# Output projection of a gated MLP: seven half-size block products per pair of token tiles, replaced by plain products

## The chip, the cores and the metric

The kernel runs on one core of a Trainium2 chip. Its time is the device time of one execution in microseconds (us); before the change it is 233.87 us, the median of three runs (233.48 to 234.02). A core has a matrix engine (TensorE, PE in the profile), three engines for elementwise work (VectorE is DVE, ScalarE is ACT, GpSimd is POOL), and SyncE (SP), which here only issues DMA transfers. The engines run side by side and wait for one another through semaphores. TensorE multiplies a 128x128 stationary block by a moving block of up to 512 columns and adds the result up in PSUM, which has eight banks of 128 x 512 fp32.

## The reference, cut to what matters

S = 2048 tokens, D = 512, gate width Fh = 896. The first half is a linear attention block, the second a gated MLP with a spatial mixing matrix:

```python
x = A_x
h = x + A_ref(layernorm(x), A_wqkv, A_wo)           # linear attention, 32 heads of 16
# B_ref(layernorm(h), ...):
z  = gelu(einsum('bsd,df->bsf', x, w_in))           # [S, 2*Fh]
z1 = z[..., :Fh]
z2 = layernorm(z[..., Fh:])
g  = einsum('ts,bsf->btf', w_sp, z2) + b_sp[None, :, None]
return einsum('bsf,fd->bsd', z1 * g, w_out)         # the output projection
# result: h + B_ref(layernorm(h), ...)
```

The change concerns the last line alone: [2048, 896] times [896, 512], added to h.

## The kernel before

The kernel is a list of operations for the five engines, each with what it reads and writes. Dependencies and semaphores are worked out from these. The order on each engine comes from a packed string, `ORDER`, which lists all operations in one fixed sequence that was found for this version of the kernel.

The output is made in 16 token tiles of 128 rows. Fh = 896 is KF = 7 contraction chunks of 128, so a plain tile takes seven products with a 512-column moving operand. The kernel before does only two of the 16 tiles plainly (`mo`). The other 14 are done two at a time (`mo_pair`). A pair, two halves of D and two groups of contraction chunks make a 2x2 by 2x2 block product; it is computed with seven block products in place of eight, by the Winograd form of Strassen's scheme. Each block product has 256 columns. HF = 3 chunks (or 2, parameter `nk`) are in each block; the rest of the seven chunks is done plainly.

The scheme needs sums and differences of blocks of the weights (`wout_sums`) and of the gated activations (`z1_sums`), made on VectorE. Partial products that go into two outputs are carried from one half of a bank to another by a ScalarE copy:

```python
def z1_sums(j, tg, nk, n):
    ...
    combine(us[0], x21, x22, ALU.add)
    combine(us[1], us[0], x11, ALU.subtract)
    combine(us[2], x11, x21, ALU.subtract)
    combine(us[3], x12, us[1], ALU.subtract)
    return us

def mo(n, banks):                                     # one tile, plain
    w = D // len(banks)
    for j, b in enumerate(banks):
        ...
        parts = ((0, 3, 6, 1, 4), (2,), (5,))
        for i, fcs in enumerate(parts):
            matmuls(bank(b, w), [(z1T[:, fc, n * P:(n + 1) * P], wout[:, fc, cs]) for fc in fcs], ...)
        dve(lambda v, o=o, b=b: v.tensor_tensor(o, bank(b, w), o, ALU.add), ...)
        store(n, cs, o, "SP" if j == 0 else "ACT")

def mo_pair(tg, i, us, nk, X, Y, tm):                 # two tiles, banks X and Y
    ...
    matmuls(X0, [(z1T[:, c, ta], wout[:, c, d0]) for c in ks])
    matmuls(X1, [(u1[:, c, ti], v1[:, c, :]) for c in ks], **onto)
    act(Y1, X0, ACT.Copy, DH2)
    for t, n in zip(tm, (a, b)):
        dve(lambda v, t=t, n=n: v.tensor_tensor(t, X1, h[:, n, d1], ALU.add), ...)
    matmuls(X0, [(z1T[:, HF + c, ta], wout[:, HF + c, d0]) for c in ks], **onto)
    matmuls(Y1, [(u2[:, c, ti], v2[:, c, :]) for c in ks], **onto)
    act(X1, Y1, ACT.Copy, DH2)
    matmuls(Y1, [(u3[:, c, ti], v3[:, c, :]) for c in ks], **onto)
    act(Y0, Y1, ACT.Copy, DH2)
    matmuls(X1, [(u4[:, c, ti], wout[:, HF + c, d1]) for c in ks], **onto)
    matmuls(Y0, [(z1T[:, HF + c, tb], v4[:, c, :]) for c in ks], **onto)
    rest = [(2 * HF,)] if nk == HF else [(2 * HF,), (HF - 1,), (KF - 2,)]
    for fcs in rest:
        for q, t in ((X, ta), (Y, tb)):
            matmuls(bank(q), [(z1T[:, fc, t], wout[:, fc, :]) for fc in fcs], **onto)
    # then four VectorE additions of 256 columns into h, and two stores
```

The projection follows the spatial mixing, which runs in two passes `p`. Each pass makes the gated activations of two groups of four tiles (`tg = p` and `p + 2`), itself with seven block products in place of eight (`cell`, 512 columns each), on PSUM banks 0 to 5:

```python
for p in range(NG // 2):
    ... # last chunk (banks 4 and 5), sums t1, t2, t4 on VectorE, three cells
    if p == 0:
        wout_sums()
        for j, tg in enumerate((0, 2)):
            us = z1_sums(j, tg, HF, 2)
            for i in (0, 1):
                mo_pair(tg, i, us, HF, 6, 7, tmp[0])
us = z1_sums(3, 3, HF - 1, 2)
mo_pair(3, 0, us, HF - 1, 6, 7, tmp[0])
mo_pair(3, 1, us, HF - 1, 0, 1, tmp[1])
us = z1_sums(2, 1, HF - 1, 1)
mo_pair(1, 0, us, HF - 1, 2, 3, tmp[2])
mo(5, (4,))
mo(7, (5, 6))
```

At its start the kernel keeps TensorE busy with products of a zero block, whose results are not used: 34 at once, and 16 more behind the statistics of the first x tile. The program with the change has these too, in the same form.

Of the kernel before, what the change touches and what calls it, by code (L numbers as in the profile page):

```python
# [6 lines left out]
FP32 = mybir.dt.float32  # L7
# [4 lines left out]
P = 128  # L12
GRAN = 16
EARLY = 1
SEM_NS = 45.0
ORDER = "c-jrogMttU00qE@tj)G<d$VoZwz=81ZQHhO+jiZ}FH8U;Aqt`)I$|IuVj(u-pq}C*0RSQ#Lc$1!;0TQ{2mv8HA|f)PA}*335t1S?k|8-#ASH4k4{{?fQXwDmqYx^h0Mep7Dxm@zp$Xz4AyT6-(x3=3pdiwr7&0L}0+A6#kr|EA6qQj0&Cnbz(E?SG1zC{|HIN;}(G}fM0zJ?TB~cAIP#rZ<8*NYvtxyVeP#0rR8f7pJV=*4}P#;UM6wA;SIZ+nn&>pSP4n5Heeb5`B5CLH^0TVF^lhGdo&=>tM1s%`;4KWA<F%5&!5zEmD2XP385riQ)f)!YaRalLqIEE8Aj^P-Abr^{?IE_&ljj5Q9&gg=fn1T6NfLS<+g;<ZZIE6EKhUa*R7kG-<n1i7hh7H(=MOchY*n#cXj4hapdDw%!*oj@(jdM7Qeb|o!*otkqiYqve3%H0&xQWZShFiFf8+eUZc!RgNjeEF{JGhGn2+oHH!H|r=06s!QzQcPw#uNO+Cw#yUe8gvb!7qHpH^ks~{6S3q`@g)t8Ym1yF)Twf79%qfqcAGtF*f5e4#P7Xe<Ky6F*P$Y53?{j^D;jRFb&f(9n&)dGcps+tRxFEA4{<`|3b{h?99QO3}hh|W)T);E(T*w)?ryDU^&KTLM~wo7Gnw4Wi2LR875|VR$xU|VoTOzZB}L#)@K7YWFt1_V&>)=u4QZXVs}<$b+%z|E@fM`ViPuF4>nYBmSl1!WfCT13Z`Uo?co-tP*3h<A1>n*4rOY!V|#YsKCa__PGw3pWi{4db2d^MrP6vH;4pS%CoX4Su3$fQ<py?Uf3D;J4&)#PF}*S<tuiZ}wlbrpa|APKII}3LvTGZ&DW`HMmvSqwy0EcEas~&p8;7uonyQ(atA$#smGUT`@~fZ<sE`6xSfe<NGg(B%bcRJ$Ld8`|C3TjiRYpg6ly`WAcX^C&SWZ{@gxC0%<yBTs`G<e`j9>Vb-?*KlxskKDgF88!b2yjtxQSypmg6{{tGJ5?xsVe$pVxVuhj@dNc#rRRj^}xwhk28?c$=Gff+zW&7x;nCd5RzTf-m`r-}#UK_v!(E@F5p*0Vi`JE2)CQtD+*PvRW&d+NiDCsl7U=qdKXxx~PhRD}(~{nX9>*5%rT7`HQdkn~x|x=4n<_JXKXl#a9j0RCOiLYhGd~MN&dtW;8`tBE^suT45Ack(F3U6h*-lQ?Zm(;S^P|6-RN^Uv*SVGqg&*)kgy~NK-UeGgVhXnysPgs^RLU?pmu68mQG8qG1}Pahk4?nyT^Yrw!_%zUrxITBie=pt+i*(dwmn8l(AIpoJQ%Ihv?RO5({{qNQ4-Wm>O|+N{OeqHU_J<=U<_+N7;op_SU9ojRx#-m4SZrG473BRZ<%I;oUCrFcH9LprV9+M_f2pks>fq&}y!I<H*5pi8=<)K1{*x~6o#sLQ&etGcUOx~Y50?Sy`ykNT|p`lMt|<VSj_w0^8-dZHIf<yU&G41TKTdZ{n^s&{&;^!}#r`k};5<1EhVU;3$x{;hxdBl@rMI=O>6o9#@7<<Jh}0uJdA4(rSg=kU(&07r0kM|2biI+`Onvhz5HV>qYtIjW;OjtjZ43%aO_IHpUun2Wov>$#yDxuj#ev75N5OS`#yx|f@|tjoBCd%M2-x`F$+rCYhb`?<B-xUC0xpa*%d%ejJsJk&$n&J|tB<z3lTT-~KS!BsuclU>7;T+_8&&9&X$9o*5w-N~KZ#ob-UQ#{qvJj@%t$(udWBRtD9Jl&(c#oav0<2=?gy~eXW$Md|_>pa&ByvR$u-t)cCi@ns#z09k;(%Zb<JG|336w1N<UT+lFU42_y9m``p-aWj*E4<pf{2yF?$Zh"


class _Op:
# [233 lines left out]
def bass_sequential_preLN__linear_attn_block__mixer_gmlp__prompt_kernel(  # L253
# [14 lines left out]
    H = 32  # L268
# [115 lines left out]
    def bank(b, n=512, lo=0):  # L384
        return psum[:, b, lo:lo + n]
# [8 lines left out]
    def matmuls(out_ap, pairs, start=True, stop=True, onto=False, **k):  # L394
        n = out_ap.free_size() if callable(getattr(out_ap, "free_size", None)) else out_ap.shape[-1]

        kw = {"skip_group_check": True} if onto else {}

        def fn(pe):
            inst = None  # L400
            for i, (a, b) in enumerate(pairs):
                inst = pe.matmul(out_ap, lhsT=a, rhs=b, start=start and i == 0, stop=stop and i == len(pairs) - 1, **kw)  # L402
            return inst
        return PE(fn, [a for p in pairs for a in p], [out_ap], len(pairs) * max(65.0, n / 2.4 + 2.5), **k)
# [26 lines left out]
    def dma(eng, out_ap, in_ap, name, issue=100.0, lat=2500.0, **k):  # L431
        return g.add(eng, lambda q: q.dma_start(out_ap, in_ap), [in_ap], [out_ap], cost=issue, lat=lat, dma=name, **k)  # L432
# [406 lines left out]
    for i, t in enumerate(order):  # L839
        w = NT // 2 if EARLY <= i < NT // 2 else NT  # L840
        for j in range(0, NT, w):
# [5 lines left out]
                first_xt.soft.add(op.i)  # L847


    EB = [4, 5]  # L850
    DH2 = D // 2
    rows = lambda r, n, hi, half: wsp[:, r:r + n, hi * S // 2 + half * DH2:hi * S // 2 + (half + 1) * DH2]
    v1, v2, v3, v4 = (rows(0, HF, hi, half) for hi in (0, 1) for half in (0, 1))
    tmp = [[g.sbuf(f"tmp{b}{j}", o_wsp + (r * S + j * S // 2) * 2, [DH2], FP32) for j in (0, 1)]
           for b, r in enumerate((NT - 1, 11, 14))]

    def wout_sums():
        y11, y12, y21, y22 = (wout[:, c:c + HF, d:d + DH2] for c in (0, HF) for d in (0, DH2))
        combine(v1, y12, y11, ALU.subtract)
        combine(v2, y22, v1, ALU.subtract)  # L860
        combine(v3, y22, y12, ALU.subtract)
        combine(v4, y21, v2, ALU.subtract)

    def z1_sums(j, tg, nk, n):
        us = [rows(HF + j * HF, nk, hi, half)[:, :, 0:n * P] for hi in (0, 1) for half in (0, 1)]
        x11, x12, x21, x22 = (z1T[:, c:c + nk, tg * GW + t:tg * GW + t + n * P] for t in (0, DH2) for c in (0, HF))
        combine(us[0], x21, x22, ALU.add)
        combine(us[1], us[0], x11, ALU.subtract)
        combine(us[2], x11, x21, ALU.subtract)
        combine(us[3], x12, us[1], ALU.subtract)  # L870
        return us

    def store(n, cs, o, eng="SP"):
        nm = f"o{n}{cs.start}"
        dma(eng, out_d[n * P:(n + 1) * P, cs], o, nm, issue=600, lat=2000)
        g.final.append(nm)

    def mo(n, banks):
        w = D // len(banks)
        for j, b in enumerate(banks):  # L880
            cs = slice(j * w, (j + 1) * w)
            o = h[:, n, cs]
            parts = ((0, 3, 6, 1, 4), (2,), (5,))
            for i, fcs in enumerate(parts):
                matmuls(bank(b, w), [(z1T[:, fc, n * P:(n + 1) * P], wout[:, fc, cs]) for fc in fcs],
                        start=i == 0, stop=i == len(parts) - 1)
            dve(lambda v, o=o, b=b: v.tensor_tensor(o, bank(b, w), o, ALU.add), [bank(b, w), o], [o], w, ps=True)
            store(n, cs, o, "SP" if j == 0 else "ACT")

    def mo_pair(tg, i, us, nk, X, Y, tm):  # L890
        u1, u2, u3, u4 = us
        a, b = tg * TPG + i, tg * TPG + i + 2
        ta, tb = slice(a * P, (a + 1) * P), slice(b * P, (b + 1) * P)
        d0, d1 = slice(0, DH2), slice(DH2, D)
        X0, X1, Y0, Y1 = (bank(q, DH2, lo) for q in (X, Y) for lo in (0, DH2))
        ks, ti = range(nk), slice(i * P, (i + 1) * P)
        onto = dict(start=False, onto=True)
        matmuls(X0, [(z1T[:, c, ta], wout[:, c, d0]) for c in ks])
        matmuls(X1, [(u1[:, c, ti], v1[:, c, :]) for c in ks], **onto)
        act(Y1, X0, ACT.Copy, DH2)  # L900
        for t, n in zip(tm, (a, b)):
            dve(lambda v, t=t, n=n: v.tensor_tensor(t, X1, h[:, n, d1], ALU.add), [X1, h[:, n, d1]], [t], DH2, ps=True)
        matmuls(X0, [(z1T[:, HF + c, ta], wout[:, HF + c, d0]) for c in ks], **onto)
        matmuls(Y1, [(u2[:, c, ti], v2[:, c, :]) for c in ks], **onto)
        act(X1, Y1, ACT.Copy, DH2)
        matmuls(Y1, [(u3[:, c, ti], v3[:, c, :]) for c in ks], **onto)
        act(Y0, Y1, ACT.Copy, DH2)
        matmuls(X1, [(u4[:, c, ti], wout[:, HF + c, d1]) for c in ks], **onto)
        matmuls(Y0, [(z1T[:, HF + c, tb], v4[:, c, :]) for c in ks], **onto)
        rest = [(2 * HF,)] if nk == HF else [(2 * HF,), (HF - 1,), (KF - 2,)]  # L910
        for fcs in rest:
            for q, t in ((X, ta), (Y, tb)):
                matmuls(bank(q), [(z1T[:, fc, t], wout[:, fc, :]) for fc in fcs], **onto)
        for n, q0, q1, t in ((a, X0, X1, tm[0]), (b, Y0, Y1, tm[1])):
            for o, q, add in ((h[:, n, d0], q0, h[:, n, d0]), (h[:, n, d1], q1, t)):
                dve(lambda v, o=o, q=q, add=add: v.tensor_tensor(o, q, add, ALU.add), [q, add], [o], DH2, ps=True)
            store(n, slice(0, D), h[:, n, :])

    cnt = [0, 0]

# [6 lines left out]
    def combine(out_ap, a, b, op):  # L927
        n = out_ap.shape[1] * out_ap.shape[2]
        return dve(lambda v: v.tensor_tensor(out_ap, a, b, op), [a, b], [out_ap], n, acc=2)
# [23 lines left out]
    for p in range(NG // 2):  # L953
# [12 lines left out]
        for k in range(HF):  # L966
# [5 lines left out]
                combine(s4, x12, s2, ALU.subtract)  # L972
                combine(x21, x11, x21, ALU.subtract)
            cell(k, lo, hi)
        if p == 0:
            wout_sums()
            for j, tg in enumerate((0, 2)):
                us = z1_sums(j, tg, HF, 2)
                for i in (0, 1):
                    mo_pair(tg, i, us, HF, 6, 7, tmp[0])  # L980
    us = z1_sums(3, 3, HF - 1, 2)
    mo_pair(3, 0, us, HF - 1, 6, 7, tmp[0])
    mo_pair(3, 1, us, HF - 1, 0, 1, tmp[1])
    us = z1_sums(2, 1, HF - 1, 1)
    mo_pair(1, 0, us, HF - 1, 2, 3, tmp[2])
    mo(5, (4,))
    mo(7, (5, 6))

    g.schedule()
    g.emit()  # L990
# [29 lines left out]
```

## Time and profile before

| what | before |
|---|---|
| time, median of 3 | 233.87 us (233.48 to 234.02) |
| span of the profiled execution | 232.1 us, 3230 instructions |
| TensorE busy | 224.1 us (97%), 1180 instructions |
| VectorE busy | 159.8 us (69%), 323 instructions |
| ScalarE busy | 103.8 us (45%), 193 instructions |
| 128x256 products of the output projection recorded | 50 + 54 + 18 + 18 |
| VectorE additions that end a tile or carry a part (lines 887, 902, 916) | 0.8 + 0.7 + 5.5 + 5.8 + 5.7 us |
| ScalarE copies of 128x256 inside PSUM | 21, 7.6 us |

A row of the groups of instructions gives the source line, the engine and operation, what is written from what, the shape, the count, the busy time and the mean duration of one. Products of a matrix engine overlap, so the mean duration of one (379 ns with 512 columns) is longer than the distance between two starts; the distance is read from the timeline. Some product records can be missing from a trace, a few in a hundred; the weight loads, one for each product, help to count.

### The profile page before, as it was taken

How to read it: one execution, taken by the hardware profiler on the slowest of the kernel's cores; microseconds unless marked ns; L12 is line 12 of the kernel's file. 1: busy time of each engine (PE TensorE's matmuls, PEld its weight loads, DVE VectorE, ACT ScalarE, POOL GpSimd, SP SyncE). 2: the span in 40 equal slices, each digit the busy share in tenths (PEclk: the TensorE clock that was granted, in tenths of full speed). 3: DMA queues.
4: the chain of work that ended last, by engine and by line, in shares of the span. 5: the costliest groups of instructions: out<-in, count | busy, mean ns of one | idle time of the engine just before them, and what ended most of it. 6: DMA issues, size and time to landing. Idle time of an engine off the chain costs nothing.

```text
span 232.1 us, 3230 instructions
## 1 busy us (share of the span) xinstructions
PE 224.1 (97%) x1180; PEld 110.4 (48%) x1203; DVE 159.8 (69%) x323; ACT 103.8 (45%) x193; POOL 45.0 (19%) x134
## 2 busy tenths in 40 slices
PE   7699999999999999999999999999999999999995
PEld 7344444453344443455444444444455555555453
DVE  3699855637898820129679996688797695582595
ACT  5586654389869687689762010112111212013110
POOL 3354300000665500726851000000000000000000
PEclk9999999999999999999999999999999999999999
DMA  6894339937457469939999300000000002000015
GB/s 189 262 206 91 57 60 336 340 72 182 110 98 156 95 131 146 186 78 212 176 226 222 73 3 0 0 0 0 3 0 24 0 3 90 0 24 3 0 45 181
DMA packets 58864, 23.68 MB, mean 102 GB/s; under 512 B 48480, under 2 KB 58720, under 8 KB 58848
## 3 DMA queue, kind: packets, MB, share of 16 engines
q1 hardware_dynamic: 58144, 22.88, 44.8%
q10 hardware_dynamic: 704, 0.59, 0.8%
q8 instruction: 9, 0.15, 0.3%
q14 instruction: 7, 0.06, 0.1%
HBM read 7.47 MB, written 2.10 MB: 41 GB/s over the span
## 4 chain that ended last, share of the span: by engine, by line
PE 89%; DVE 3%; DMA 3%; POOL 2%; issue 1%; ACT 1%; SPq 1%; DVEq 0%
PE psum L402 70%; PE psum L655 6%; PE psum L802 6%; PE psum L805 4%; DMA x<-in_A_x_dram 3%; DVE st L511 1%; POOL rs L551 1%; PE psum L751 1%; SPq L432 1%; ACT m L421 0%; POOL st L535 0%; PE psum L720 0%; PE psum L676 0%; DVE xn L556 0%; PE psum L685 0%
## 5 line engine op out<-in xcount | busy, mean ns | idle before, releaser
L421 ACT ACTIVATE psum<-psum 128x256 f32<-128x256 f32 (+1 forms) x33 | 14.4, 445 | 91.6 <-PE psum L402 42.5
L402 PE MATMUL psum<-wsp,z 128*128 128x512 bf16 x203 | 47.1, 379 | 0.3
L402 PEld LDWEIGHTS psum<-wsp,z 128*128 128x128 bf16 x208 | 20.3, 98 | 23.1 <-ACT psum L421 0.5
L402 PE MATMUL psum<-hnT,win 128*128 128x512 bf16 x109 | 25.3, 379 | 0.2
L402 PE MATMUL psum<-t,s 128*128 128x512 bf16 x94 | 22.2, 379 | 0.1
L421 ACT ACTIVATE e<-psum 128x1024 bf16<-128x1024 f32 (+1 forms) x18 | 16.7, 927 | 12.5 <-PE psum L402 12.0
L421 ACT ACTIVATE z1T<-psum 128x512 bf16<-128x512 f32 x28 | 16.3, 594 | 4.9 <-PE psum L402 4.9
L924 DVE TENSOR_TENSOR u<-psum,bsp 128x512 bf16<-128x512 f32 x16 | 11.0, 687 | 10.2 <-PE psum L402 7.5
L421 ACT ACTIVATE z<-psum 128x896 bf16<-128x896 f32 x16 | 14.5, 914 | 4.1 <-PE psum L805 4.1
L402 PEld LDWEIGHTS psum<-hnT,win 128*128 128x128 bf16 x112 | 9.9, 98 | 13.5 <-ACT z1T L421 4.1
L402 PE MATMUL psum<-wout,z1T 128*128 128x256 bf16 (+1 forms) x82 | 16.3, 314 | 0.0
L802 PE MATMUL psum<-win,hnT 128*128 128x512 bf16 x63 | 16.2, 379 | 0.1
L402 PE MATMUL psum<-wqkv,xnT 128*128 128x512 bf16 x62 | 14.9, 379 | 0.9 <-ACT xnT L421 0.8
L556 DVE TENSOR_SCALAR hn<-h,st,rs 128x512 bf16<-128x512 bf16 x16 | 6.0, 407 | 13.7 <-POOL rs L547 13.2
L402 PE MATMUL psum<-xnT,wqkv 128*128 128x512 bf16 x61 | 15.1, 379 | 0.2
L655 PE MATMUL psum<-pk,xn 128*128 128x512 bf16 x63 | 15.2, 379 | 0.1
L402 PE MATMUL psum<-m,pqT 128*128 128x512 bf16 x62 | 14.7, 379 | 0.4 <-DVE h L776 0.3
L402 PEld LDWEIGHTS psum<-t,s 128*128 128x128 bf16 x96 | 9.4, 98 | 10.4
L511 DVE BATCH_NORM_STATS2 st<-x 128x6 f32<-128x512 bf16 x15 | 9.9, 677 | 5.0 <-DMA x<-in_A_x_dram 5.0
L776 DVE SCALAR_TENSOR_TENSOR h<-psum,x 128x512 bf16<-128x512 f32 x16 | 10.5, 682 | 4.0 <-PE psum L402 4.0
L805 PE MATMUL psum<-win,hnT 128*128 128x384 bf16 x64 | 13.0, 326 | 0.0
L582 DVE TENSOR_SCALAR e<-e 128x1024 bf16<-128x1024 bf16 (+1 forms) x18 | 7.0, 391 | 7.9 <-ACT e L421 7.7
(113 smaller groups left out, 348.6 us busy)
## 6 DMA issues: line engine op xcount, KB each, us to landing
r<-rcp SPq DMA_DIRECT2D x16, 128.0 KB, 2.7
out_dram<-h SPq DMA_DIRECT2D x15, 128.0 KB, 1.8
win<-in_B_w_in_dram SPq DMA_DIRECT2D x2, 896.0 KB, 8.6
x<-in_A_x_dram SPq DMA_DIRECT2D x6, 256.0 KB, 4.8
wqkv<-in_A_wqkv_dram SPq DMA_DIRECT2D x2, 512.0 KB, 8.6
wout<-in_B_w_out_dram SPq DMA_DIRECT2D x1, 896.0 KB, 8.0
wo<-in_A_wo_dram SPq DMA_DIRECT2D x1, 512.0 KB, 4.1
bsp<-in_B_b_sp_dram SPq DMA_DIRECT2D x1, 512.0 KB, 4.8
```

Of the source, the lines that this page charges most:

```text
L402: inst = pe.matmul(out_ap, lhsT=a, rhs=b, start=start and i == 0, stop=stop and i == len(pairs) - 1, **kw)
L421: return g.add("ACT", lambda ac: ac.activation(out_ap, in_ap, func, **kw), [in_ap, *extra], [out_ap] + ([accum] if accum is not None else []),
L432: return g.add(eng, lambda q: q.dma_start(out_ap, in_ap), [in_ap], [out_ap], cost=issue, lat=lat, dma=name, **k)
L511: dve(lambda v: v.bn_stats(s[:, 0:6], src[:, n, :]), [src[:, n, :]], [s[:, 0:6]], D)
L551: pool(lambda p: p.tensor_tensor(r, ve, expo[:, 0:1], ALU.pow), [ve, expo], [r], 620)
L556: return dve(lambda v: v.tensor_scalar(dst, src, mean, rst, op0=ALU.subtract, op1=ALU.mult), [src, mean, rst], [dst], w + 460, acc=4)
L582: dve(lambda v: v.tensor_scalar(e, e, 1.0, EPS_PHI, op0=ALU.min, op1=ALU.add), [e], [e], w * GW, acc=4)
L655: inst = pe.matmul(bank(CB[c]), lhsT=xn[:, i, c * P:(c + 1) * P], rhs=pk[:, i, :], start=i == 0, stop=i == NT - 1)
L776: dve(lambda v, n=n, b=b, s=s: v.scalar_tensor_tensor(h[:, n, :], bank(b), 1.0, x[:, n, :], op0=ALU.mult, op1=ALU.add, accum_out=s[:, 0:1] ...
L802: pe.matmul(bank(b), lhsT=hnT[:, c, n * P:(n + 1) * P], rhs=win2[:, c, 0:GW], start=c == 0, stop=c == KD - 1)
L805: inst = pe.matmul(bank(b + 1, F2), lhsT=hnT[:, c, n * P:(n + 1) * P], rhs=win2[:, c, GW:FH], start=c == 0, stop=c == KD - 1)
L924: dve(lambda v: v.tensor_tensor(t, bank(b), add, ALU.add), [bank(b), add], [t], GW, ps=True)
```

## The change

Sums, pairs, temporaries and copies are dropped, and all 16 tiles are done plainly. Tiles of pass 0 alternate between banks 6 and 7; those of pass 1 go round banks 6, 7, 4 and 5. The last tile is done in two halves of 256 columns, so that the end of the kernel is short. The point of a plain projection is that the operands stay as they are: no sums on VectorE, no copies inside PSUM, and fewer, larger products, for one more block product in eight.

```diff
-    def wout_sums(): ...                  # four sums of weight blocks
-    def z1_sums(j, tg, nk, n): ...        # four sums of activation blocks
-    def mo(n, banks): ...
-    def mo_pair(tg, i, us, nk, X, Y, tm): ...
+    EB, MB = [4, 5], [6, 7, 4, 5]
+
+    def mo(n, nb):
+        w = D // 2 if n == NT - 1 else D
+        for j in range(0, D, w):
+            b, cs = MB[n % nb] if j == 0 else 0, slice(j, j + w)
             o = h[:, n, cs]
             parts = ((0, 3, 6, 1, 4), (2,), (5,))
             for i, fcs in enumerate(parts):
                 matmuls(bank(b, w), [(z1T[:, fc, n * P:(n + 1) * P], wout[:, fc, cs]) for fc in fcs],
                         start=i == 0, stop=i == len(parts) - 1)
             dve(lambda v, o=o, b=b: v.tensor_tensor(o, bank(b, w), o, ALU.add), [bank(b, w), o], [o], w, ps=True)
-            store(n, cs, o, "SP" if j == 0 else "ACT")
+            dma("SP" if j == 0 else "ACT", out_d[n * P:(n + 1) * P, cs], o, f"o{n}{j}", issue=600, lat=2000)
...
-        if p == 0:
-            wout_sums()
-            for j, tg in enumerate((0, 2)):
-                ...                        # four pairs
-    us = z1_sums(3, 3, HF - 1, 2)
-    ...                                    # three pairs, mo(5, (4,)), mo(7, (5, 6))
+        for tg in (p, p + NG // 2):
+            for n in range(tg * TPG, (tg + 1) * TPG):
+                mo(n, 2 + 2 * p)
```

The string `ORDER` is another one too, since the list of operations is another: it also moves operations of the earlier stages against each other. For instance, the load of the value weights (`wv`, a third of `wqkv`) is now issued behind one of the transposing loads of `w_sp`, and the attention output products (`m`, `pqT`) are mixed in another way with the first products of the MLP.

More of the change, by code (lines that the diff above doesn't have):

```diff
@@ L15 @@
 SEM_NS = 45.0
-ORDER = "c-jrogMttU00qE@tj)G<d$VoZwz=81ZQHhO+jiZ}FH8U;Aqt`)I$|IuVj(u-pq}C*0RSQ#Lc$1!;0TQ{2mv8HA|f)PA}*335t1S?k|8-#ASH4k4{{?fQXwDmqYx^h0Mep7Dxm@zp$Xz4AyT6-(x3=3pdiwr7&0L}0+A6#kr|EA6qQj0&Cnbz(E?SG1zC{|HIN;}(G}fM0zJ?TB~cAIP#rZ<8*NYvtxyVeP#0rR8f7pJV=*4}P#;UM6wA;SIZ+nn&>pSP4n5Heeb5`B5CLH^0TVF^lhGdo&=>tM1s%`;4KWA<F%5&!5zEmD2XP385riQ)f)!YaRalLqIEE8Aj^P-Abr^{?IE_&ljj5Q9&gg=fn1T6NfLS<+g;<ZZIE6EKhUa*R7kG-<n1i7hh7H(=MOchY*n#cXj4hapdDw%!*oj@(jdM7Qeb|o!*otkqiYqve3%H0&xQWZShFiFf8+eUZc!RgNjeEF{JGhGn2+oHH!H|r=06s!QzQcPw#uNO+Cw#yUe8gvb!7qHpH^ks~{6S3q`@g)t8Ym1yF)Twf79%qfqcAGtF*f5e4#P7Xe<Ky6F*P$Y53?{j^D;jRFb&f(9n&)dGcps+tRxFEA4{<`|3b{h?99QO3}hh|W)T);E(T*w)?ryDU^&KTLM~wo7Gnw4Wi2LR875|VR$xU|VoTOzZB}L#)@K7YWFt1_V&>)=u4QZXVs}<$b+%z|E@fM`ViPuF4>nYBmSl1!WfCT13Z`Uo?co-tP*3h<A1>n*4rOY!V|#YsKCa__PGw3pWi{4db2d^MrP6vH;4pS%CoX4Su3$fQ<py?Uf3D;J4&)#PF}*S<tuiZ}wlbrpa|APKII}3LvTGZ&DW`HMmvSqwy0EcEas~&p8;7uonyQ(atA$#smGUT`@~fZ<sE`6xSfe<NGg(B%bcRJ$Ld8`|C3TjiRYpg6ly`WAcX^C&SWZ{@gxC0%<yBTs`G<e`j9>Vb-?*KlxskKDgF88!b2yjtxQSypmg6{{tGJ5?xsVe$pVxVuhj@dNc#rRRj^}xwhk28?c$=Gff+zW&7x;nCd5RzTf-m`r-}#UK_v!(E@F5p*0Vi`JE2)CQtD+*PvRW&d+NiDCsl7U=qdKXxx~PhRD}(~{nX9>*5%rT7`HQdkn~x|x=4n<_JXKXl#a9j0RCOiLYhGd~MN&dtW;8`tBE^suT45Ack(F3U6h*-lQ?Zm(;S^P|6-RN^Uv*SVGqg&*)kgy~NK-UeGgVhXnysPgs^RLU?pmu68mQG8qG1}Pahk4?nyT^Yrw!_%zUrxITBie=pt+i*(dwmn8l(AIpoJQ%Ihv?RO5({{qNQ4-Wm>O|+N{OeqHU_J<=U<_+N7;op_SU9ojRx#-m4SZrG473BRZ<%I;oUCrFcH9LprV9+M_f2pks>fq&}y!I<H*5pi8=<)K1{*x~6o#sLQ&etGcUOx~Y50?Sy`ykNT|p`lMt|<VSj_w0^8-dZHIf<yU&G41TKTdZ{n^s&{&;^!}#r`k};5<1EhVU;3$x{;hxdBl@rMI=O>6o9#@7<<Jh}0uJdA4(rSg=kU(&07r0kM|2biI+`Onvhz5HV>qYtIjW;OjtjZ43%aO_IHpUun2Wov>$#yDxuj#ev75N5OS`#yx|f@|tjoBCd%M2-x`F$+rCYhb`?<B-xUC0xpa*%d%ejJsJk&$n&J|tB<z3lTT-~KS!BsuclU>7;T+_8&&9&X$9o*5w-N~KZ#ob-UQ#{qvJj@%t$(udWBRtD9Jl&(c#oav0<2=?gy~eXW$Md|_>pa&ByvR$u-t)cCi@ns#z09k;(%Zb<JG|336w1N<UT+lFU42_y9m``p-aWj*E4<pf{2yF?$Zh"
@@ new lines @@
+ORDER = "c-jTQ17HvU6a>(_`)OOX)wZ^{TC0W{Ggl2Qj@h<t+qP}nwr$&Xz2}T{aD_WEzyqGh1~0fEJ=~B5#ZUyrQ4|1SNQP8!fFqJ41%#Z)0UvlH7jh#HeBp-@D2Y<2g1m@B8N?zU4bd1`ksbaBKsbVs52X=_vIs#SA`pxy<VPr)pb-*~h^A<U=4gR1Bq16FP#pzP6@^d@El~rtP!qM$8s*UqT~H2P(H$|!h)l?gx@v_ssDp8+fQqP#dKix}7>gxXhNW1J!l;DGXp45}ft2WpUg(Vpn25=kgcV2)C#=M3q`@krMIZD<KlDd^G{681M0<2VM;yc<9L5n$!xRj{U<|=g9K&&(zz7V-8jQp!jK(^g#&k?YCv?V4%)kQ7$1E(wNvy?soWV1k!gIXD3)It7%*GrH#V~Bd1}ws2Y{Cv~$7XE7T+G8B?8Q#(!fu?yS?t4p9Kcp=!&O|td0fCn+{7hZ#x>l+b=<&fyu};5!fo8cUEIeVJVbInKnkX0T0Vj^UHA^~@fc6=1E25#Kk*qK@eN<#LGT}b;VZu559-T_4s>KHdNL!^GacRN$}~*P-}nnZ`ZJWpSdsyBX9k9`6f-dkvobUDG9LpO#9)?ZagzCIEWvP!6<B};S%`(1j5Sz^wHd-9%*M*}Vo_%25;kW|wqix*pf{_q7E7}X%QAwIjA9+uWjS`^8n$K&_GB*RW;A2y!<<~qrCiHp+`=~8%598g9P6<@8?Yhc*@y{DWNz(Y9_?jIHsw0@ViJ8>jd|FZQ|Pbt?9QniL0=8!FpgwfwqtvC;Bt0k7xrLp2FOp%Sd|Ubgbh`lfy%2s?8|=a&jB3BecaCj9LykvDxZQiiXjTqbmmt<&0ql)QehQU5f#@=7SnK+&@>)lNrmeukFk_Ws}l!t2s^VYM{^7hax7<YHs^30k8?YB@B~kCE;n!^4{<!_aRpCtA<u9ECviT@sH`FsrAU=iw8|?+XIViNb%$42Nq2dbl~qO8_=ZpTmQVSIfBB5}c$(*Up4Zt(jnza=)l3t)fQvYp_xXS~xQRFUkdOF|@A-ij_?Rnsk(c<KmwA}~2vIM%iaYs|uegi1c$=%ao16KO(kI3%R$rK)I3+5LzA{PQm{!T<EElCy3Z>L{{-CM4vMRk?l}ZkB)K6xUm$EB|y!DGtYOWS)sa$HM)@q}+YNz(<ppNRK&Z;4IWsry5<f)8$&Cg7&oXVuk@=-EnQB~DeHPuut{pJ+)Q!n*bZw=5Y4blt^RvpdMP|a2s4Odrn(+G{!R87|qjnXuY(_9VHc&*iHP0&2eS9kSLANABgEzlCp(mIXSLiN=c&Cys*)Fe&TQf<(BZPXeq(lTw<a&6KUZPj9J({`=UO6|~29o1g#(|#S(0UgvK9oH@$)(M@`X`Rto?baTh*9BeF6<yUeUD8e6(rsPW9o^G?J<wx4(NlfWJH6LOCAZH?VPBQXzRS^G>xJIvtzPPte(0G#=!;U?Fa6Uu{S?f>ev9@;59MTO%)?}9EuE#dzcNc^&gNq2&CNV5lewF#Ww5N4&B83u@>`H)F)zz#*)6l>FmLm-+~#kEEsqs3Ukk9jR@91FuobX^meYJJmsPY9R>>+`Nh@X1R?cFqiiKDiD{B!JZsje`;w`}<Ezxf1r0y!8J=YNxvdb!Nj}&U>6l<lef<;-9{Rc`Ukl6"
@@ L847, in bass_sequential_preLN__linear_attn_block__mixer_gmlp__prompt_kernel @@
                 first_xt.soft.add(op.i)
[L850 to L881, printed above, removed]
+    EB, MB = [4, 5], [6, 7, 4, 5]
[3 more added lines that the diff above has]
+            b, cs = MB[n % nb] if j == 0 else 0, slice(j, j + w)
             o = h[:, n, cs]
@@ L887, in mo @@
             dve(lambda v, o=o, b=b: v.tensor_tensor(o, bank(b, w), o, ALU.add), [bank(b, w), o], [o], w, ps=True)
-            store(n, cs, o, "SP" if j == 0 else "ACT")
[L890 to L917, printed above, removed]
+            dma("SP" if j == 0 else "ACT", out_d[n * P:(n + 1) * P, cs], o, f"o{n}{j}", issue=600, lat=2000)
+            g.final.append(f"o{n}{j}")
     cnt = [0, 0]
@@ L974, in bass_sequential_preLN__linear_attn_block__mixer_gmlp__prompt_kernel @@
             cell(k, lo, hi)
-        if p == 0:
-            wout_sums()
-            for j, tg in enumerate((0, 2)):
-                us = z1_sums(j, tg, HF, 2)
-                for i in (0, 1):
-                    mo_pair(tg, i, us, HF, 6, 7, tmp[0])
-    us = z1_sums(3, 3, HF - 1, 2)
[L982 to L987, printed above, removed]
+        for tg in (p, p + NG // 2):
+            for n in range(tg * TPG, (tg + 1) * TPG):
+                mo(n, 2 + 2 * p)
     g.schedule()
```

## The prediction

> **What bounds the kernel now.** I read the busy times first, then the slices, to see whether one engine is full over the whole span or only on average.
>
> ```profile
> PE 224.1 (97%) x1180; PEld 110.4 (48%) x1203; DVE 159.8 (69%) x323; ACT 103.8 (45%) x193; POOL 45.0 (19%) x134
> ...
> PE   7699999999999999999999999999999999999995
> ...
> DVE  3699855637898820129679996688797695582595
> ACT  5586654389869687689762010112111212013110
> ...
> PEclk9999999999999999999999999999999999999999
> ```
>
> TensorE is at 9 tenths or more in every slice but the first two and the last, at full clock throughout. VectorE has full slices but never governs for long; ScalarE is nearly idle in the second half. Since ends of products are modelled, a busy row alone is no proof, so next I asked what TensorE waited for.
>
> ```profile
> PE psum L570 <- DVE xn L556: 1.4, 3, 0.6
> PE psum L594 <- POOL warm L439: 1.0, 1, 1.0
> PE psum L402 <- ACT xnT L421: 0.8, 1, 0.8
> PE psum L402 <- DVE h L776: 0.3, 1, 0.3
> PE psum L751 <- DVE pqT L585: 0.3, 1, 0.3
> PE psum L570 <- DVE pk L587: 0.2, 1, 0.2
> ```
>
> These are all its waits (total us, times, longest). Those on L570, L594 and xnT belong to the start, the other two to the attention's end. None is in the mixing or the projection. A count of product starts gives the same. The chain of waits gives the distance of two 512-column starts, and the timeline of the end that of two 256-column starts:
>
> ```profile
> 69.35 3.45 PE psum L402 x16
> ```
>
> ```profile
> 207.90 0.38 PE L402 MATMUL psum<-wsp 128*128 128x256 bf16 x2
> 208.12 0.38 PE L402 MATMUL psum<-wout,z1T 128*128 128x256 bf16 x2
> 208.34 0.38 PE L402 MATMUL psum<-wsp 128*128 128x256 bf16 x2
> 208.56 0.38 PE L402 MATMUL psum<-wout,z1T 128*128 128x256 bf16 x2
> ```
>
> 3.45 / 16 = 0.2156 us for 512 columns; 0.22 / 2 = 0.110 us for 256. So half the columns cost 51% of the time: the scheme's small products lose almost nothing. From the first mixing product (the timeline has it at 120.59 us) on, the program holds 400 products of 512 columns for the mixing, and for the projection of before: four pairs with 3 chunks, 4 x (21 of 256 + 2 of 512); three pairs with 2 chunks, 3 x (14 of 256 + 6 of 512); tile 5, 7 of 512; tile 7, 14 of 256. That is 140 of 256 and 33 of 512. Together 400 x 0.2156 + 140 x 0.110 + 33 x 0.2156 = 86.2 + 15.4 + 7.1 = 108.7 us, so without a stall the last start period would end at 120.6 + 108.7 = 229.3 us. The chain's end shows how near that is:
>
> ```profile
> 224.71 4.08 PE psum L402 x23
> 228.79 0.02 issue
> 228.81 0.76 DVE h L916 x2
> 229.57 0.01 issue
> 229.57 0.42 DVE h L887
> ```
>
> The last addition (of 256 columns, line 887) starts at 229.57, which is 229.3 plus the drain of the last product (0.273 - 0.110 = 0.16, from the 256-column mean of the groups) plus about 0.1 for the semaphore. So the last 109 us are a TensorE stream with practically no holes, and the time is the sum of its products.
>
> **What the Trainium skill says.** "TensorE: Matmul & The Clock Gate", section Back-to-back issue gap, gives N/2.4 + 2.5 ns for a warm product on its own, so 215.8 ns at 512 and 109.2 at 256; the trace agrees (215.6 and 110). The same section says that a stream of loads and products sustains about 131 ns at 512 columns; this trace, a stream of just that kind, does not show it, and I use 215.6. "VectorE: DVE Perf Modes", section The perf-mode tier table, says that an elementwise operation of two tensors runs at twice the base rate on bf16 in SBUF and at the base rate with an operand in PSUM. The trace agrees: 419 ns for the gate's product in SBUF against 687 ns for its sum out of PSUM, both of 512 elements. "PSUM — Partial Sum Buffer", section The four PSUM rules, says that VectorE and ScalarE writes do not touch the bits that make a product accumulate, so a product can add onto copied data where an earlier product has set them; the pairs' copies and `onto` rest on that. No time depends on it here.
>
> **The change, part by part.**
>
> Removed on TensorE: 140 x 0.110 + 33 x 0.2156 = 15.40 + 7.11 = 22.51 us. Added: 15 plain tiles x 7 = 105 of 512, and the last tile as 14 of 256: 22.64 + 1.54 = 24.18 us. Net **+1.67 us**, all in the stretch without holes, so all on the path.
>
> Removed on VectorE: 28 additions of line 916 (5.8 + 5.7), 14 of line 902 (5.5), three of line 887 (0.8 + 0.7), and 20 block sums: 12 of 768 elements (12 x 0.55 = 6.6), 4 of 512 (1.7), 4 of 256 (1.1). Sum 27.9 us. Added: 15 x 0.69 + 2 x 0.42 = 11.2 us (0.69 is the one 512-column addition of line 887). VectorE loses 16.7 us, and ScalarE its 21 copies, 7.6 us. None of this is on the path while TensorE has other products to run; what it can return is the holes that it causes. Weight loads, which can wait while an earlier product runs, waited 1.1 us for the PSUM copies of ScalarE over the whole kernel, and no product did. I count **0**.
>
> The end: before, the last product is followed by a 256-column addition (0.42) and a 64 KB store issued by ScalarE (1.6 us to landing). In the new order, the last seven products are again of 256 columns, then a 256-column addition and a 64 KB store by ScalarE. The tile just before is of 512 columns: its addition can start 7 x 0.110 = 0.77 us earlier than the last and takes 0.69, so it is done in time. **0**.
>
> The earlier stages: the operations are the same, the order is not. From 14.3 to 120.6 us I count 352 products of 512 columns outside the z stage (75.9 us), 64 couples of 512 and 384 columns in it (the chain has 0.86 + 0.65 us for four, so 64 x 0.378 = 24.2), and 4.4 us of small products: 104.5 in 106.3 us. So at most 1.8 us is to be won there, and it is about as easily doubled. I put **+0.1** for it.
>
> Sum: 233.87 + 1.67 + 0.1 = 235.6 us.
>
> **The rivals.**
>
> Relief of VectorE and ScalarE: 16.7 and 7.6 us less might let gates, copies and sums come sooner. For it speaks that VectorE has 9 tenths in some slices of the second half; against it, that no product waited for it there. The most it can return is about 1 us: 234.6.
>
> Fewer instructions: 119 products in place of 173. Had each a fixed cost beside its columns, 54 fewer would pay. But 2 x 0.110 - 0.2156 = 0.004 us, and the pair count above has it already.
>
> Two banks for pass 0: tiles alternate between banks 6 and 7, so a tile's products wait until the addition of the tile before last is done. A tile takes 7 x 0.2156 = 1.51 us, an addition 0.69 with some 0.2 of drain and semaphore. It fits if VectorE is free, and fails if one of the large sums (2.28 us each) for pass 1 comes between. In the new order six of the eight additions stand before these sums, and the last two tiles of pass 0 need no bank back soon. If it failed, one or two tiles would wait 1 to 2 us: 237 to 238.
>
> Pass 1's sums come late: they stand behind the sixth addition. At that time TensorE has two tiles (14 products) and 32 mixing products left before it needs the second sum: 46 x 0.2156 = 9.9 us, against 0.9 + 2 x 2.28 = 5.5 us. It fits with 4 us to spare.
>
> Earlier stages worse: the value weights were issued at 36.02 us, landed 11.7 us later (47.7) and are needed at 50.94. Now a transposing load of `w_sp`, which held the queue 5.64 us at that place, goes ahead. If the issue slips that far and the landing with it, to 53, TensorE waits about 2 us; but the transfers share one backlog that drained at about 46 us, so I expect it to land before 51. The result with such a wait would be 237 to 238.
>
> **Range and chances.** The +1.67 rests on counts and on two distances that agree within 2 ns; I trust it to 0.1. Runs differ by 0.3. The rest is in the order: between -0.8 (relief, or a better early order) and +1 (one wait). This gives 234.6 to 236.7. Faster by 2% would need less than 229.3, which no part offers: 0.01. Slower by 2% needs 238.5, so 2.9 us of new waits beside the sum, more than any one of the rivals brings: 0.04. Within 2%: 0.95.
>
> **What would show it.** Right: in the changed profile, products of 512 columns from w_out number about 105, starts stay 0.216 us apart, and the stretch from the first mixing product to the last addition is 1.7 us longer. VectorE's busy time falls by about 16 us and ScalarE's by 7 without effect. Wrong, if TensorE shows waits for `h` additions between the tiles of pass 0, for `t` sums early in pass 1, or for `wqkv` near 51 us; or if the first mixing product starts more than 0.5 us earlier or later than at 120.6. If the stretch of the mixing and the projection is no longer than before, the distance of the small products misled me.

## The result, and the profile after

The changed kernel takes 235.31 us (median of six runs, 234.76 to 235.93) against 233.88 us (233.48 to 234.02) for the kernel before in the same session: a ratio of 1.0066 with a 95% interval of 1.0048 to 1.0083. So it is slower by about 1.4 us of 234, and well inside 2%.

The page of the changed kernel: first the busy time of each engine, then the slices of the span.

```profile
PE 225.5 (97%) x1127; PEld 105.4 (45%) x1149; DVE 148.0 (63%) x275; ACT 97.3 (42%) x172; POOL 43.6 (19%) x134
...
PE   7799999999999999999999999999999999999995
...
DVE  4799756637988540266599978584578019851464
ACT  5695753489989778778851000010001000100000
...
PEclk9999999999999999999999999999999999999999
```

TensorE has 53 recorded instructions fewer than before and is busy 1.4 us longer. VectorE has lost 11.8 us and ScalarE 6.5 us of busy time, and the span has not gained from it: the row of TensorE has its 9 in every slice but the first two and the last, just as before.

All waits of TensorE in the changed kernel (us in total, times, longest):

```profile
PE psum L570 <- DVE xn L556: 1.6, 4, 0.8
PE psum L594 <- POOL warm L439: 1.0, 1, 1.0
PE psum L402 <- ACT xnT L421: 0.7, 1, 0.7
PE psum L402 <- DVE h L776: 0.2, 1, 0.2
```

Again only the start and the end of the attention stand here. There is no wait for the additions into `h` at the end of a projection tile (line 861), none for the sums of pass 1 and none for `wqkv`. The `h` of line 776 is the sum after the attention.

The stretch that the prediction counted, from the first mixing product to the start of the last addition, is therefore what to measure. The table of stretches gives the stretch and its length, and for PE, PEld, DVE, ACT and POOL the busy time and the instructions, then the granted clock, the DMA share and GB/s. For the kernel before:

```profile
120.59:229.57 108.98, 108.37 (x563) 55.51 (x572) 84.31 (x154) 15.45 (x35) 1.72 (x4) 1.00 0.14 35
```

And for the changed one:

```profile
119.76:230.49 110.73, 110.16 (x510) 50.59 (x518) 71.81 (x108) 8.09 (x14) 1.90 (x4) 1.00 0.19 44
```

The stretch grew by 1.75 us, and TensorE's busy time in it by 1.79. VectorE lost 12.5 us inside it and ScalarE 7.4. The first mixing product started 0.83 us earlier, which is why the span of this profile is only 0.9 us longer. That start varies from run to run (below), and the profiled execution happened to be the fastest of the six.

The groups of instructions of the changed kernel (count | busy us, mean ns | idle before, and what ended it) show the projection as it now is:

```profile
L402 PE MATMUL psum<-wout,z1T 128*128 128x512 bf16 x102 | 23.5, 379 | 0.1
...
L402 PEld LDWEIGHTS psum<-wout,z1T 128*128 128x128 bf16 x119 | 11.6, 98 | 12.8 <-DVE z1T L871 0.7
...
L861 DVE TENSOR_TENSOR h<-psum,h 128x512 bf16<-128x512 f32 x15 | 10.0, 686 | 5.9 <-PE psum L402 5.9
...
L402 PE MATMUL psum<-wout,z1T 128*128 128x256 bf16 x14 | 2.0, 273 | 0.0
```

The 119 weight loads are the 105 + 14 products of the program; three product records are missing. The products idled 0.1 us in all. The 5.9 us in the row of additions is VectorE waiting for TensorE, not the reverse.

The end, in the chain of waits of the changed kernel (start us, us, what):

```profile
224.99 5.48 PE psum L402 x29
230.46 0.02 issue
230.49 0.42 DVE h L861
```

As before, the chain is products until 0.02 us ahead of one 256-column addition. The tail has neither grown nor shrunk.

### The profile page after: what moved, and what is told of

Same layout as the page of the kernel before. It is cut to its first block, busy times and chain, and to the rows that moved or that the text cites. A ratio compares the mean times of both kernels' runs of the same rounds, so it can differ in the third digit from the quotient of the medians.

```text
span 233.0 us, 3045 instructions
## 1 busy us (share of the span) xinstructions
PE 225.5 (97%) x1127; PEld 105.4 (45%) x1149; DVE 148.0 (63%) x275; ACT 97.3 (42%) x172; POOL 43.6 (19%) x134
## 4 chain that ended last, share of the span: by engine, by line
PE 87%; DMA 5%; DVE 3%; ACT 2%; SPq 1%; issue 1%; POOL 1%; ACTq 0%; DVEq 0%
PE psum L402 69%; PE psum L802 6%; PE psum L655 6%; PE psum L805 4%; DMA x<-in_A_x_dram 2%; DMA hnT<-hn 1%; DMA r<-rcp 1%; DVE st L511 1%; SPq L742 1%; SPq L432 1%; ACT pqT L421 0%; PE psum L676 0%; DVE xn L556 0%; PE psum L685 0%; ACT sh L421 0%
## 5 line engine op out<-in xcount | busy, mean ns | idle before, releaser
L402 PE MATMUL psum<-wsp,z 128*128 128x512 bf16 x205 | 46.5, 379 | 0.2
L421 ACT ACTIVATE psum<-psum 128x512 f32<-128x512 f32 x12 | 7.0, 582 | 86.6 <-DVE u L870 49.8
L402 PE MATMUL psum<-wout,z1T 128*128 128x512 bf16 (+1 forms) x116 | 25.0, 366 | 0.1
L421 ACT ACTIVATE e<-psum 128x1024 bf16<-128x1024 f32 (+1 forms) x18 | 16.7, 927 | 13.9 <-PE psum L402 13.7
L402 PE MATMUL psum<-t,s 128*128 128x512 bf16 x93 | 21.7, 379 | 0.2
L402 PEld LDWEIGHTS psum<-wout,z1T 128*128 128x128 bf16 x119 | 11.6, 98 | 12.8 <-DVE z1T L871 0.7
L402 PE MATMUL psum<-m,pqT 128*128 128x512 bf16 x63 | 15.2, 379 | 0.3 <-DVE h L776 0.2
L861 DVE TENSOR_TENSOR h<-psum,h 128x512 bf16<-128x512 f32 (+1 forms) x17 | 10.7, 655 | 6.7 <-PE psum L402 6.6
```

The lines of the kernel that those rows point to most:

```text
L421: return g.add("ACT", lambda ac: ac.activation(out_ap, in_ap, func, **kw), [in_ap, *extra], [out_ap] + ([accum] if accum is not None else []),
```

## The experiments

The theory: the time is the sum of TensorE's products in the last 109 us, so only their number and width count. The rivals: fewer and larger products save something per instruction; VectorE's relief returns time; the additions hold up pass 0; the moved order of the earlier stages is what matters.

### The changed kernel again, and the two orders exchanged

The string `ORDER` changed with the list of operations, so the change has two parts: another projection, and another order in the earlier stages. These three runs part them. The first has no edit. The other two change only `ORDER`: all operations ahead of the mixing stand in the sequence of the other kernel.

```diff
 # after's projection, before's order of the earlier stages; and the reverse
-ORDER = "c-j..."
+ORDER = "c-j..."    # places of the operations ahead of the mixing from the other kernel
```

> The changed kernel once more, unaltered. In its first trace the first mixing product started at 119.76 us, 0.83 us earlier than before (120.59); 0.34 of that is x tiles landing earlier, which no part of the change explains. Theory A (product count plus order): the stretch from the first mixing product to the last addition is 110.7 us again, the median 235.3. If the landing of x is chance, the first mixing product starts at 119.8 to 120.3. Rival B (relief of VectorE and ScalarE returns time in the last stretch): the stretch is shorter than the 110.6 that the products make by more than 0.3 us.

> The changed kernel with the operations ahead of the mixing in the order of the kernel before; mixing and plain projection in the new order. Theory A, order of the front worth about 0.45 us: median 235.7 to 235.8, first mixing product at 120.2 to 120.6, last stretch 110.7. Rival C (the early gain was chance of the landing): same as the changed kernel, 235.3.

> The kernel before (pairs) with the operations ahead of the mixing in the order of the changed kernel. Theory A: the last stretch stays at 109.0 us and the front gains 0.45: 233.4, faster than both. Rival C: 233.9. Rival B says nothing of it.

| kernel | projection | earlier order | median us | ratio to before (95%) | first mixing product | stretch |
|---|---|---|---|---|---|---|
| before | pairs | before | 233.88 | | 120.59 | 108.98 |
| changed | plain | after | 235.31 | 1.0066 (1.0048 to 1.0083) | 119.76 | 110.73 |
| changed, again | plain | after | 235.36 | 1.0074 (1.0054 to 1.0093) | 120.43 | 110.73 |
| orders exchanged | plain | before | 235.52 | 1.0068 (1.0048 to 1.0089) | 120.61 | 110.72 |
| orders exchanged | pairs | after | 233.72 | 0.9993 (0.9979 to 1.0007) | 120.77 | 109.12 |

The stretch follows the projection: 110.72 or 110.73 us for every plain one, 108.98 and 109.12 for the pairs. It repeats to 0.01 us where the start of the stretch moves by 0.8. So the whole loss belongs to the projection. The 0.14 us between the two kernels with pairs are one hole in the mixing of the second. There a weight load waited for a ScalarE copy inside PSUM, which had itself waited for VectorE:

```profile
134.36 0.38 PE L402 MATMUL psum<-t,s 128*128 128x512 bf16 x1
...
134.69 0.13 PEld L402 LDWEIGHTS psum<-wsp,s 128*128 128x128 bf16 x2 [0.45 <-ACT psum L421]
134.72 0.38 PE L402 MATMUL psum<-wsp,s 128*128 128x512 bf16 x1
```

The two products start 0.36 us apart in place of 0.216. The list of waits does not show this, because the second product starts before the recorded end of the first.

The order of the earlier stages is worth 0.16 us in the medians, in both comparisons (235.52 - 235.36, 233.88 - 233.72). This is not shown to differ from zero: in the first the two intervals overlap, and the ratios even put it the other way round (1.0074 against 1.0068); in the second the interval holds 1. The expected 0.45 us is not shown either: 235.52 lies between what the two theories said, and 233.72 nearer to 233.9 than to 233.4. The first profile had made me expect more: its mixing began 0.83 us earlier. The start of the chain of waits shows one reason. This is the landing of an early load of x (256 KB, behind four smaller loads of x) before the change,

```profile
2.19 6.07 DMA x<-in_A_x_dram
```

and this in the changed kernel:

```profile
2.19 5.73 DMA x<-in_A_x_dram
```

These 0.34 us are chance: the issue is at the same place in both programs, and in the ten profiles of this study that piece lies between 5.18 and 6.35 us. The first products behind it move along (those of `pk,xn` start between 12.17 and 13.41 us), but later waits can hide it: in the second run of the changed kernel this piece took 5.64 us, and the mixing still began at 120.43, since a product waited 0.62 us for `xnT` at 18.9. A second reason is in the timeline of TensorE at the end of the attention (start us, us, engine, line, operation, and in brackets the wait ahead of it). In the changed kernel:

```profile
64.00 0.40 PE L751 MATMUL psum<-pqT,zc 128*32 128x512 bf16 x4
64.46 1.04 PE L802 MATMUL psum<-win,hnT 128*128 128x512 bf16 x4
```

With the pairs behind the same early order:

```profile
64.47 0.40 PE L751 MATMUL psum<-pqT,zc 128*32 128x512 bf16 x4
65.46 1.04 PE L802 MATMUL psum<-win,hnT 128*128 128x512 bf16 x4 [0.59 <-DMA hnT<-hn]
```

The first product of the MLP follows 0.46 us behind the start of the last attention row in one and 0.99 in the other, since its transposing load had not landed. The landing of x (6.06 us) was that of the profile before (6.07), where the same product started at 65.29. Without the wait it would have started at 65.46 - 0.59 = 64.87, so the new order asks for `hnT` 0.42 us sooner, and in this run the load took all of it back. Among the six profiles with after's early order, three have this wait (0.35 to 0.69 us). Over all ten profiles the first mixing product stands at a mean of 120.16 with after's order and 120.61 with before's. That is 0.45 us, which the medians do not confirm. Sign and size of the order's effect on the time stay open.

### Every wide product of the projection as two narrow ones

If products had a fixed cost each, this kernel with 105 products more would show it. The operands and results stay the same.

```diff
+                if halves:                        # only where the tile has 512 columns
+                    for lo in (0, n // 2):
+                        s = slice(lo, lo + n // 2)
+                        inst = pe.matmul(out_ap[:, s], lhsT=a, rhs=b[:, s], start=start and i == 0 and lo == 0, ...)
+                    continue
```

> The changed kernel with every 512-column product of the projection made as two 256-column products with the same weights: 105 more products, the same columns, the same VectorE work. If a 256-column product costs 0.110 us against 0.2156, as read from the starts: plus 105 x 0.0044 = 0.46 us, so 235.8. Rival D (small products have a hidden fixed cost, so that the pairs' gain should have been smaller than counted, and part of the plain products' price is only that): 20 ns or more each, plus 2 us or more, 237.4.

Measured: 235.51 us, ratio 1.0078 (1.0056 to 1.0099). The stretch:

```profile
119.83:230.82 110.99, 110.95 (x625) 60.94 (x623) 71.77 (x108) 8.09 (x14) 1.89 (x4) 1.00 0.19 43
```

It is 0.26 us longer than that of the changed kernel (110.73). 105 more products for 0.26 us is 2.5 ns each, so a product of 256 columns costs (215.6 + 2.5) / 2 = 109 ns in a stream, a little less than the 110 that I took from two rounded starts. The rival of "fewer instructions" falls, and rival D with it: removing 54 instructions saves 54 x 2.5 ns = 0.13 us, while the extra columns cost more than ten times that. Half-size block products lose about 1% to their size.

### One product in seven done twice

The dose: is the stretch really the sum of its products, so that an added one counts in full? The first product of each sum is done once more ahead of itself (15 of 512 columns, 2 of 256; the second one starts the sum anew, so the result stays the same).

```diff
+                if twice and i == 0:              # the first product of each sum of mo
+                    pe.matmul(out_ap, lhsT=a, rhs=b, start=True, stop=True)
```

> The changed kernel with the first product of each tile's sum made twice, the second overwriting the first: 15 more products of 512 columns and 2 of 256, no more VectorE work. Theory A (the stretch is the sum of its products): plus 15 x 0.2156 + 2 x 0.110 = 3.45 us, 238.8. If TensorE had waits in the stretch that could take them up, less.

Measured: 238.54 us (median of four), ratio 1.0206 (1.0189 to 1.0223). The stretch:

```profile
119.63:233.81 114.18, 114.14 (x537) 52.34 (x535) 71.87 (x108) 8.09 (x14) 1.89 (x4) 1.00 0.18 43
```

It grew by 114.18 - 110.73 = 3.45 us. Expected from 15 x 0.2156 + 2 x 0.110 is 3.45. Nothing absorbs a product in this stretch. Had there been hidden slack, the dose would have shown less than its sum.

### The block sums cut, with the pairs kept

This takes VectorE's relief alone. In the kernel before, each of the 20 block sums is computed on 8 columns of each chunk only, with the rest of the pairs as it was. The sums are thus incomplete and the output is not the reference's; only the time is of use.

```diff
-    def combine(out_ap, a, b, op):
+    def combine(out_ap, a, b, op, w=None):        # w = 8 for wout_sums and z1_sums
+        c = slice(0, w or out_ap.shape[2])
-        return dve(lambda v: v.tensor_tensor(out_ap, a, b, op), ...)
+        return dve(lambda v: v.tensor_tensor(out_ap[:, :, c], a[:, :, c], b[:, :, c], op), ...)
```

> The kernel before with its 20 block sums on VectorE cut to 8 columns per chunk, so about 8 us less VectorE work in the last 70 us; the sums are left incomplete, so only its time is of use. Theory A: nothing, 233.9 within 0.2. Rival B (relief of VectorE returns up to 1 us): 232.9 to 233.4.

Measured: 233.82 us (14 runs), ratio 0.9987 (0.9970 to 1.0004). The stretch:

```profile
120.86:229.84 108.98, 108.94 (x574) 55.68 (x572) 78.51 (x155) 15.45 (x35) 1.72 (x4) 1.00 0.17 38
```

VectorE is busy 5.8 us less than before (84.31), and the stretch is 108.98 us, the same to the hundredth. So this part of the relief is worth nothing. The copies and the pairs' additions were not taken away by themselves, because the products need them; for them the starts of the products give a bound. In the whole stretch of the kernel before, one place has starts further apart than the products' own distance (a missing record leaves twice the distance, and no more):

```profile
216.35 0.38 PE L402 MATMUL psum<-wout,z1T 128*128 128x512 bf16 x1
216.59 0.11 PEld L402 LDWEIGHTS psum<-wsp,z 128*128 128x128 bf16 x2 [0.36 <-ACT psum L421]
216.59 0.39 PE L402 MATMUL psum<-wsp,z 128*128 128x512 bf16 x1
```

The two starts are 0.246 us apart, and the next one follows after 0.227, in place of 0.216 each. So in this stretch at most 0.04 us could have come back, whatever VectorE and ScalarE were spared. The copy waited for here has 512 columns, so it is one of the mixing; those of the pairs have 256.

### Four of the seven pairs made plain

If the loss is the sum of products, half of the change must bring its share. The four pairs of pass 0 are replaced by eight plain tiles on banks 6 and 7, with the three pairs of pass 1 and the order of the earlier stages kept.

```diff
-            for j, tg in enumerate((0, 2)):
-                us = z1_sums(j, tg, HF, 2)
-                for i in (0, 1):
-                    mo_pair(tg, i, us, HF, 6, 7, tmp[0])
+            for tg in (0, 2):
+                for n in range(tg * TPG, (tg + 1) * TPG):
+                    mo(n, (6 + n % 2,))
```

> The kernel before with its four pairs of pass 0 (3 chunks) done as eight plain tiles on banks 6 and 7; the three pairs of pass 1 and all else as before, and the front in the order of before. With the cost of a small product from the halves run, (0.2156 + 0.0025) / 2 = 0.109 us, each of these pairs saves 14 x 0.2156 - 21 x 0.109 - 2 x 0.2156 = 0.298 us. Theory A: the stretch grows by 4 x 0.298 = 1.19 us to 110.2, and the median to about 235.1. Rival E (the price of the change lies in pass 1 or the tail, not in the products alike): 233.9 to 234.3.

Measured: 234.91 us (13 runs), with 233.91 for the kernel before beside it, ratio 1.0050 (1.0031 to 1.0068). The stretch:

```profile
120.39:230.56 110.17, 109.61 (x528) 52.06 (x536) 76.98 (x130) 11.21 (x23) 1.72 (x4) 1.00 0.15 36
```

The stretch grew by 1.19 us, 0.298 for each pair: 14 x 0.2156 = 3.018 for two plain tiles against 21 x 0.109 + 2 x 0.2156 = 2.720 for the pair. The chain's end of this kernel shows that the tail of the pairs is unchanged:

```profile
224.50 5.27 PE psum L402 x32
229.78 0.02 issue
229.80 0.76 DVE h L916 x2
230.55 0.01 issue
230.56 0.42 DVE h L887
```

### The additions split in four

The rival of the two banks says that in pass 0 a slower addition would be felt. Here each 512-column addition is done as four of 128 columns.

```diff
-            dve(lambda v, ...: v.tensor_tensor(o, bank(b, w), o, ALU.add), ...)
+            for c in range(j, j + w, e):          # e = 128 where the tile has 512 columns
+                inst = v.tensor_tensor(h[:, n, c:c + e], bank(b, e, c - j), h[:, n, c:c + e], ALU.add)
```

> The changed kernel with each 512-column addition that ends a tile done as four of 128 columns. Same results and waits, but VectorE holds each bank longer, by an estimate of about 0.3 to 0.5 us (four short additions, each with a fixed part). Theory A: a tile of 1.51 us leaves room, so the stretch stays at 110.7 and the median at 235.3 to 235.4. Rival F (two banks in pass 0 are nearly binding): waits for h appear between tiles, six tiles times some tenths, 236 to 237.

Measured: 235.58 us (7 runs), ratio 1.0061 (1.0039 to 1.0083). The timeline of VectorE in pass 0 of the changed kernel (the bracket is its idle time and what ended it):

```profile
167.66 0.69 DVE L861 TENSOR_TENSOR h<-psum,h 128x512 bf16<-128x512 f32 x1 [2.16 <-PE psum L402]
...
169.33 0.68 DVE L861 TENSOR_TENSOR h<-psum,h 128x512 bf16<-128x512 f32 x1
170.68 0.69 DVE L861 TENSOR_TENSOR h<-psum,h 128x512 bf16<-128x512 f32 x1 [0.67 <-PE psum L402]
172.19 0.69 DVE L861 TENSOR_TENSOR h<-psum,h 128x512 bf16<-128x512 f32 x1 [0.82 <-PE psum L402]
172.80 2.28 DVE L875 TENSOR_TENSOR t<-wsp 128x4096 bf16<-128x4096 bf16 x1
```

And with the additions split:

```profile
170.30 0.88 DVE L864 TENSOR_TENSOR h<-psum,h 128x128 bf16<-128x128 f32 x4
171.46 0.88 DVE L864 TENSOR_TENSOR h<-psum,h 128x128 bf16<-128x128 f32 x4 [0.29 <-PE psum L402]
172.97 0.88 DVE L864 TENSOR_TENSOR h<-psum,h 128x128 bf16<-128x128 f32 x4 [0.63 <-PE psum L402]
173.77 2.28 DVE L880 TENSOR_TENSOR t<-wsp 128x4096 bf16<-128x4096 bf16 x1
```

In both, VectorE stands idle ahead of the additions with a bracket and waits for TensorE, which delivers a tile every 1.51 us (170.68 to 172.19, and 171.46 to 172.97). A tile's addition takes 0.69 or 0.88 us, and the other bank has its products meanwhile. No product is held up by an addition: from the first to the last product start it is 110.4 us in both kernels, the same to the nanosecond. The stretch is 110.76 us; the 0.03 more lie at its end, where the last addition stands behind the four pieces of the tile before. The rival falls, at this size of addition. It is a weaker test than was planned, since the bank is held 0.19 us longer and not 0.3 to 0.5. A longer addition, or a sum of 2.28 us between two additions, was not tried.

## Why the prediction was right, point by point

**The products, +1.67 us.** Right, and a little small: the stretch grew by 1.75, or 1.74 before rounding. The term that was mis-sized is the price of the 256-column product. At the 109 ns of the split products, the sum is 22.64 + 14 x 0.109 - (140 x 0.109 + 33 x 0.2156) = +1.79. The 0.04 between this and the stretch are the late starts at 216.6 us in the kernel before, shown above. The formula that the Trainium skill gives for a product on its own in "TensorE: Matmul & The Clock Gate", section Back-to-back issue gap, comes to 109.2 ns at 256 columns and agrees. The sustained 131 ns at 512 columns of the same section is not seen here: 15 added products of 512 and 2 of 256 brought 3.45 us, which leaves about 215 ns for each wide one.

**VectorE and ScalarE, worth 0.** Right in its effect: cutting 5.8 us of VectorE's sums changed the stretch by 0.00, and the starts leave 0.04 us for all of it. That no product was held up by a PSUM copy was wrong by these 0.04. The size was off for VectorE: I summed durations to 16.7 us. The recorded durations in the stretch did fall by 16.8 us (93.4 to 76.6), but its busy time by 12.5. Durations of neighbours overlap: two 256-column additions of 0.42 us take 0.76 together in the chain's end above. ScalarE's 7.6 was 7.4.

**The end, 0.** Right: products until the last 256-column addition in both kernels.

**The earlier stages, +0.1.** This was a guess, and it did not come true in the six runs, at a size that does not matter for the outcome. The first mixing product came 0.83 us earlier in the first profile, more than the 0.5 I had named as a sign of being wrong; 0.34 of it is the landing of x. In the medians the new order gains 0.16 us, not shown to differ from zero. The measured +1.43 us is 0.3 less than the +1.77 of the sum. The stretch alone cost 1.75, so in those six runs the earlier stages gave back about 0.3 where I had put a cost of 0.1; 0.16 of it is the order in the medians, and the rest is within the spread of the runs (234.76 to 235.93). So this term was about 0.4 too high and that of the products 0.08 too low, which leaves the forecast of 235.6 about 0.3 above the median. The range was also added up loosely: -0.8 and +1 about 235.6 give 234.8 to 236.6, not 234.6 to 236.7; the result lies in both.

**The rivals.** Relief, two banks and fewer instructions fell in the runs above. No product of the changed kernel waited for the sums of pass 1. The value weights, which I feared might come at 53 us, were issued 3.9 us later than before. The queue that issues transfers, in the changed kernel:

```profile
35.30 4.56 SPq L435 DMA_TRANSPOSE wsp<-in_B_w_sp_dram  x1
39.91 0.58 SPq L432 DMA_DIRECT2D wqkv<-in_A_wqkv_dram  x1
```

They landed 7.4 us after their issue, at 47.3, in place of 11.7 before: a later issue by 3.9 us, a landing about half a microsecond earlier. That fits the argument of a shared backlog, which no run tested by itself. They were needed at 50.5.

## What to carry to other kernels

Where one engine's instructions stand without gaps over a long stretch, add up its instructions by the measured distance of two starts, and let relief of the other engines count for nothing until a wait for them is seen. A scheme that saves one block product in eight kept its gain on TensorE here even in blocks of 256 columns (0.298 us of 3.02 for a pair with three chunks); its sums and copies fitted beside the products, and a case where they do not was not tried. Waits shorter than the overlap of two products are found only in the distances of starts. Judge a change of order in the early stages by medians of many runs, and the stretch by the profile: here the start of the mixing lay between 119.63 and 120.86 us in ten profiles, while the stretch repeated to 0.01 where the projection was the same plain one.

## What was not expected of the hardware

- Halving a product's columns cost only 2.5 ns for each extra product, with the weight block loaded once per half (623 loads recorded against 518).
- Four additions of 128 columns out of PSUM took 0.88 us against 0.69 for one of 512: about 0.06 us for each further instruction, though one of 128 is recorded at 0.28 us alone.
- The same load at the same place in the program, 256 KB of x, lasted 5.18 to 6.35 us in ten profiles, and moved the start of the first products behind it.
